# A seven-product MLP on one Trainium2 core: second products onto a seeded PSUM bank, inner products that end by themselves, sums of w1 loaded by GpSimd

## The chip, the cores and the metric

The kernel runs on one core of one Trainium2 chip. The metric is the time of one execution in microseconds (us) on the device, over several runs. PE is TensorE (the matrix engine, PEld its weight loads), DVE is VectorE, ACT is ScalarE, POOL is GpSimd, SP is SyncE.

## The reference

Two blocks in a row, all in fp32. The first is a routed attention (4 batches, 8 heads, 768 rows, 64 columns a head, 16 clusters). The change touches only the second, an MLP with a residual for each of the 3072 rows:

```python
# x: (4, 768, 512), the output of the attention block
mu = np.mean(x, axis=-1, keepdims=True)
var = np.mean((x - mu) ** 2, axis=-1, keepdims=True)
xn = (x - mu) / np.sqrt(var + 1e-06) * g_ln
ch = np.maximum(xn @ w_ch1, 0.0) @ w_ch2     # 512 -> 2048 -> 512
return (x + ch).astype(np.float32)
```

## The kernel before

**Products.** Each matrix product of the MLP is cut into 2 x 2 blocks and done with seven products of blocks in place of eight, on sums of blocks (the scheme of Strassen and Winograd). The code calls the products "ways" or "parts" 1 to 7. Their results are put together so: block (0,0) is 1 + 2; a chain 1, 6, 7, 4 is accumulated in the PSUM bank `x`, and copied out after each step (p1, u2, u3, and the end, which is block (1,0)); 5 is in the bank `z`; block (1,1) is z + u3; 3 is accumulated onto z, and block (0,1) is z + u2. Product 2 has a bank `y` of its own, and `add_relu` (L913) or `put_in` (L1227) adds the kept p1 to it on DVE.

**Stages.** By the times of the trace: attention to 317.4 us. Batch 0 goes through the first layer to 387.3 and through a plain second layer to 462.5. Batch 1 has its first layer to 531.1; its second is "deep" to 600.6: the seven products are themselves made of seven each, 49 products (`deep_product`, L1200) of four matmuls of 192 columns. Batches 2 and 3 have a "paired" first layer (`paired_layer`, L1473; to 666.6 and 799) and a deep second layer (to 733.5 and about 862.5). The first layer's products are `first_layer` (L926), four matmul records of 384 columns each. Some of them are done by pairs of blocks with seven inner products of one matmul of 192 columns (`inner_products`, L1334); in the paired layer there are three kinds, called A, B and C in the plan, for the first, fifth and third sum.

**Order.** All of it stands in an order written out by hand for each engine (`manual_schedule`). For the first layer the tuple `parts` (L1778) gives the order of the parts of a block with what is put between them; for the deep layer `STEPS` (L1056) walks `ORDER` (4, 7, 1, 6, 5, 2, 3), and for each m the ways 1, 2, then 4 and 3 of the m before, then 6, 5, 7. The jobs that a step carries (row norms of the next batch, transposes and stores of results, ring loads of weights on SP) are hung on pairs (way, slot) and (m, way).

**PSUM and buffers.** After the attention the banks are a pool of six for `x` and `z` and one of two for the rest. The copies p1, u2, u3 of the chain are in `hid`, tag "p", five buffers. ReLU is a separate ACT instruction on what DVE has added (`relu`, L921).

**w1.** `w1_sums` (L666) makes the four sums of blocks of w1 on DVE for batch 0 and for batch 1, four adds for each of eight blocks. Batch 0's are also written to DRAM (`outer_keep`, L1373, array `w1_all`), from where the later batches load them.

## Time and profile before

| | us |
|---|---|
| runs | 872.70, 870.51, 872.72 |
| median of the runs | 872.70 |
| the profiled execution's own time | 870.29 |
| its span, first to last instruction | 868.7 |
| granted clock of PE in it | 0.999 of full |

The span is what the rows below speak of; the 1.6 us between it and the execution's own time lie around it. Times in rows are counted from the start of the span.

### The profile page before, as it was taken

Reading aid. Unit: us, or ns where it says so; the run is one execution under the profiler, and the core shown is the slowest. Engines: PE = TensorE matmul, PEld = TensorE weight load, DVE = VectorE, ACT = ScalarE, POOL = GpSimd, SP = SyncE. Lnnn points to the kernel's source line nnn. Section 1 sums busy time; section 2 is a strip of 40 time slices with the busy share of each in tenths; the row PEclk is TensorE's granted clock in tenths of the full one; section 3 lists DMA queues with packets and bytes.
Section 4 is the critical chain, followed back from the end, with each engine's and each line's share of the span. In section 5 each row is a group of like instructions: output and inputs, shape, how many; then the busy total and the mean of one; then the engine's idle time right before and its main releaser. Section 6 shows DMA issues by size and latency. Waiting matters only on the chain.

```text
span 868.7 us, 13931 instructions
## 1 busy us (share of the span) xinstructions
PE 861.5 (99%) x4827; PEld 597.5 (69%) x4827; DVE 740.1 (85%) x1304; ACT 425.9 (49%) x808; POOL 142.5 (16%) x230
## 2 busy tenths in 40 slices
PE   8999999999999999999999999999999999999997
PEld 5444444444444446668887667998778999778997
DVE  6899999999999878888977898888888897767876
ACT  6877788888888845561003543112663111344110
POOL 2011221222222223220000210002430002250000
PEclk9999999999999999999999999999999999999999
DMA  8777889999976428978695788965556975464866
GB/s 169 137 128 130 143 177 191 201 207 202 196 168 188 126 100 262 277 189 312 204 272 153 227 272 240 293 199 172 160 151 212 343 202 166 129 169 145 275 202 124
DMA packets 229866, 169.63 MB, mean 195 GB/s; under 512 B 159440, under 2 KB 180448, under 8 KB 228768
## 3 DMA queue, kind: packets, MB, share of 16 engines
q1 hardware_dynamic: 193344, 140.30, 58.8%
q0 software_dynamic: 11632, 23.95, 12.7%
q10 hardware_dynamic: 24816, 4.45, 2.9%
q8 instruction: 39, 0.64, 0.3%
q14 instruction: 35, 0.29, 0.1%
HBM read 119.67 MB, written 40.59 MB: 184 GB/s over the span
## 4 chain that ended last, share of the span: by engine, by line
PE 97%; DVE 1%; DMA 1%; issue 0%; ACT 0%; SPq 0%; ACTq 0%; DVEq 0%
PE x_ps L881 19%; PE s_ps L420 18%; PE a_ps L432 15%; PE x_ps L1216 12%; PE z_ps L1216 6%; PE x_ps L998 5%; PE z_ps L881 5%; PE x_ps L1342 5%; PE y_ps L1216 3%; PE z_ps L998 2%; PE z_ps L1342 2%; PE sim_ps L331 2%; PE den_ps L488 1%; PE y_ps L998 1%; PE y_ps L1342 1%; PE y_ps L881 1%
## 5 line engine op out<-in xcount | busy, mean ns | idle before, releaser
L420 PE MATMUL s_ps<-t,t 64*128 64x384 f32 x768 | 155.0, 483 | 0.1
L420 PEld LDWEIGHTS s_ps<-t,t 64*128 64x128 f32 x768 | 67.9, 187 | 39.1 <-issue 38.3
L1291 POOL DMA_DIRECT2D out_dram<-y x64 | 49.6, 783 | 209.1 <-DVE y L1277 183.6
L1216 PE MATMUL x_ps<-lower,w 128*128 128x192 f32 x448 | 80.5, 326 | 0.0
L1216 PEld LDWEIGHTS x_ps<-lower,w 128*128 128x128 f32 x448 | 74.2, 190 | 0.8
L412 ACT ACTIVATE e<-s_ps 128x768 f32<-128x768 f32 x83 | 66.4, 812 | 7.2 <-PE s_ps L420 6.6
L412 ACT ACTIVATE w<-s_ps 128x768 f32<-128x768 f32 x80 | 64.4, 812 | 7.9 <-PE s_ps L420 7.0
L420 PE MATMUL s_ps<-mask,mask 64*128 64x384 bf16 x384 | 62.3, 323 | 0.4 <-ACT e L412 0.4
L923 ACT ACTIVATE lower<-lower 128x384 f32<-128x384 f32 x88 | 42.9, 520 | 35.5 <-DVE lower L915 30.5
L910 ACT COPY p<-x_ps 128x384 f32<-128x384 f32 x31 | 14.7, 475 | 92.5 <-PE x_ps L881 85.6
L432 PE MATMUL a_ps<-e,v_sb 128*64 128x384 f32 x336 | 57.6, 488 | 0.0
L432 PE MATMUL a_ps<-w,v_sb 128*64 128x384 f32 x320 | 55.2, 488 | 0.0
L881 PE MATMUL x_ps<-xn,w 128*128 128x384 f32 x128 | 46.6, 487 | 0.0
L881 PE MATMUL x_ps<-xn,ws 128*128 128x384 f32 x128 | 46.6, 487 | 0.0
L881 PE MATMUL x_ps<-xt,w 128*128 128x384 f32 x128 | 46.5, 486 | 0.0
L881 PE MATMUL x_ps<-xt,ws 128*128 128x384 f32 x128 | 46.4, 486 | 0.0
L432 PEld LDWEIGHTS a_ps<-e,v_sb 128*64 128x64 f32 x336 | 23.5, 137 | 31.8 <-issue 28.7
L432 PEld LDWEIGHTS a_ps<-w,v_sb 128*64 128x64 f32 x320 | 22.4, 137 | 30.4 <-issue 27.3
L300 POOL DMA_DIRECT2D w<-tb x32 | 29.1, 908 | 80.9 <-DVE tb L297 64.4
L420 PEld LDWEIGHTS <-mask 64*128 64x128 bf16 x384 | 18.9, 94 | 33.9 <-issue 10.9
L1229 ACT COPY u<-x_ps 128x192 f32<-128x192 f32 x30 | 9.6, 319 | 65.9 <-PE x_ps L1216 61.3
L377 ACT ACTIVATE mask<-oh,far 32x384 bf16<-32x384 bf16 x61 | 37.3, 612 | 3.3 <-DVE oh L360 1.9
(346 smaller groups left out, 1893.3 us busy)
## 6 DMA issues: line engine op xcount, KB each, us to landing
w<-w_d SPq DMA_DIRECT2D x84, 256.0 KB, 3.5
raw<-in_moe_w_ch_dram SPq DMA_DIRECT2D x32, 512.0 KB, 4.9
w<-w_t SPq DMA_DIRECT2D x36, 256.0 KB, 5.0
w<-tb POOLq DMA_DIRECT2D x32, 256.0 KB, 5.4
w<-w_all SPq DMA_DIRECT2D x27, 256.0 KB, 3.5
v_sb<-in_v_dram SPq DMA_DIRECT2D x32, 192.0 KB, 3.3
xr<-x_d SPq DMA_DIRECT2D x24, 256.0 KB, 3.6
q_sb<-in_q_dram SPq DMA_DIRECT2D x62, 96.0 KB, 4.1
```

The costliest lines, as they stand in the source:

```text
L300: nc.gpsimd.dma_start(out=w, in_=fb, accum_op=ALU.add)
L331: nc.tensor.matmul(sim[r : r + Q, :HC], cT[:, pr, :, :].rearrange("p j c -> p (j c)"), prepared[n][side][:, g * HC : (g + 1) * HC], start= ...
L377: nc.scalar.activation(out, oh[src, :], AF.Identity, bias=add, scale=factor)
L412: nc.scalar.activation(e, s[2][:, :, :HC], AF.Exp, scale=SCALE)
L420: nc.tensor.matmul(s[j][:, :HC], of_keys[:, keys], of_queries[:, o : o + HC], start=part == first, stop=part != first, skip_group_check=True,)
L432: nc.tensor.matmul(acc[j * D : (j + 1) * D, :HC], loaded[n]["v"][:, j, c, :], e[:, j, :], start=(c == 0), stop=(c == NT - 1),)
L881: nc.tensor.matmul(bank[:, :HC], lhs[:, c, :], rhs[:, c], start=first and c == 0, stop=c == NDH - 1, skip_group_check=True,)
L923: nc.scalar.activation(h, h, AF.Relu)
L998: nc.tensor.matmul(bank[:, :MH].rearrange("p (h f) -> p h f", h=2), hidden[lhs + (c,)][:, tt * P : (tt + 1) * P], rhs[:, :, c], start=firs ...
L1216: nc.tensor.matmul(bank, w[:, c, :], a[:, c], start=(way in (1, 2, 5) or alone) and c == 0, stop=c == NQH - 1, skip_group_check=True,)
L1291: queues[i % len(queues)].dma_start(out=to, in_=y)
L1342: nc.tensor.matmul(bank, p["w"][way], p["x"][way], start=way in (1, 2, 5), stop=True, skip_group_check=True)
```

## The change

- Product 2 no longer has a bank of its own. A bank `seed` (pool of one) is opened once, by two bf16 matmuls that write it. After that, product 1 is copied into it (ACT; DVE adds into it where a further term belongs to it), and product 2 is accumulated onto that without a start flag. The result leaves with a copy or a ReLU on ACT. The other banks are three for `x` and four for the rest.
- In the deep layer the order of the ways becomes 1, 4 of the m before, 2, 3 of the m before, 6, 5, 7; in the first layer 4 of the block before moves ahead of 2.
- Inner products get their own sum: the block's p1 is kept in one tile for the pair (`first_kept`), the seven inner products end in the hidden tiles with ACT copies and two DVE adds, and one DVE add of 768 columns (`add_kept`) puts p1 on afterwards. In batch 3 the first two groups of the kind C still add onto what is there (`onto`), by DVE into the seed.
- For batch 1 the sums of w1 are loaded from `w1_all` on GpSimd's queue (`w1_room`, `w1_back`) instead of being made on DVE.
- `hid` "p" has three buffers, not five; `between` moves from step (4, 2) to (4, 1).

```diff
@@ PSUM pools, opening of the seed
-    pools["long"], pools["t"] = pool("ps_m", 6, space=PSUM), pool("ps_n", 2, space=PSUM)
+    seeds = pool("ps_k", 1, space=PSUM)
+    pools["chain"], pools["t"] = pool("ps_m", 3, space=PSUM), pool("ps_n", 4, space=PSUM)
+    def seeded(n):
+        return seeds.tile([P, 512], F32, tag="seed", name="seed_ps")[:, :n]
+    def open_seeded():
+        bank, parts = seeded(4 * P), ident.bitcast(BF16)
+        for i in range(2):
+            nc.tensor.matmul(
+                bank[:, i * 2 * P : (i + 1) * 2 * P], parts[:, :P], parts,
+                start=i == 0, stop=True, skip_group_check=True,
+            )
@@ first_kept, add_kept
+    def first_kept(j):
+        if j % 2 == 0:
+            ones_of["t"] = hid.tile([P, 2, HC], F32, tag="pp", name="p1", bufs=1)
+        return ones_of["t"][:, j % 2]
+    def add_kept(r, l, j, t):
+        h = place((r, l))[:, j : j + 2].rearrange("p c t -> p (c t)")
+        nc.vector.tensor_tensor(h, h, t, ALU.add)
+        summed.extend(hidden_tile(r, l * NFH + j + i) for i in range(2))
@@ first_layer
-            st["p1"] = kept(st["x"], "p1", None if b or j else w2[:, NFC - 6, :HC])
+            if j < FROM.get(b, 0):
+                st["y"] = seeded(HC)
+                nc.scalar.copy(st["y"], st["x"][:, :HC])
+            else:
+                kept(st["x"], "p1", first_kept(j))
         elif part == 2:
-            y = ps("y_ps")
-            product(y, w1_block(0, 1, j), x_block(b, 1, 0), True)
-            add_relu(0, j, y, st["p1"])
+            product(st["y"], w1_block(0, 1, j), x_block(b, 1, 0), False)
+            nc.scalar.activation(hidden_tile(0, j), st["y"], AF.Relu)
@@ STEPS
-        for way in (1, 2, 4, 3, 6, 5, 7):
-            if way not in (3, 4):
-                STEPS.append((m, way))
-            elif before:
-                STEPS.append((before, way))
+        for way in (1, 4, 2, 3, 6, 5, 7) if before else (1, 5, 6, 2, 7):
+            STEPS.append((before if way in (3, 4) else m, way))
@@ deep_product
         if way == 1:
-            kept_sum("p1", 0, 0)
+            p["y"] = seeded(QC)
+            put_in(rows_of(p["y"]), part(p["add"], 0, 0))
         elif way == 2:
-            put_in(part(p["to"], 0, 0), p["p1"])
+            put_in(part(p["to"], 0, 0), None)
@@ inner_products
+            if way == 1:
+                p["in", "y"] = seeded(QC)
...
+            if way == 1:
+                put_in(p["in", "y"], 0, 0)
+            elif way == 2:
+                nc.scalar.copy(p["to"](*at[way]), bank)
+            elif way == 4:
+                put_in(p["to"](*at[way]), *at[way])
+            elif way in (6, 7):
+                p["kept", way] = p["keep"](way)
+                put_in(p["kept", way], *{6: (0, 1), 7: (1, 1)}[way])
+            if way in (7, 3):
+                onto = p["kept", {7: 7, 3: 6}[way]]
+                nc.vector.tensor_tensor(p["to"](*at[way]), p["in", "z"], onto, ALU.add)
+    INNER = {1: (1,), 2: (2, 6, 5), 3: (7,), 4: (4, 3)}
@@ sums of w1 of batch 1, and the order of the first layer
+    def w1_back(b, j, a=0, z=4):
+        if j < NFH:
+            n = NDH * P
+            t = sets[b, j]["all"].rearrange("p s k f -> p (s k f)")
+            nc.gpsimd.dma_start(out=t[:, a * n : z * n], in_=w1_all[j, :, a * n : z * n])
...
-        parts, sums_after, inner_at = ((1, 0), (2, 0), (4, 1), (6, 0), (3, 1), (5, 0), (7, 0)), 5, {}
+        parts, sums_after, inner_at = ((1, 0), (4, 1), (2, 0), (6, 0), (3, 1), (5, 0), (7, 0)), 5, {}
...
-            inner_at = {5: (7,), 6: (4, 3)} if j % 2 else {6: (1, 2), 7: (6, 5)}
+            inner_at = {5: INNER[3], 6: INNER[4]} if j % 2 else {6: INNER[1], 7: INNER[2]}
...
-                    summed.extend(hidden_tile(0, j - i) for i in (1, 0))
+                    add_kept(0, 0, j - 1, flat(ones_of["t"]))
...
+            if b and j and part in (1, 7):
+                w1_back(b, j + 1, *{1: (0, 3), 7: (3, 4)}[part])
-            if part == (sums_after if j or b == 0 else 6) and j + 1 < NFH:
+            if b == 0 and part == sums_after and j + 1 < NFH:
                 w1_sums(b, j + 1)
```

In the rows of orders below, the number behind a name tells buffers apart; `in_ps` is a bank of inner products, `p1` the pair's kept tile, `pi` and `kept` are copies of inner products.

DVE where batch 1 goes from its first into its deep second layer, before (`z_ps_4537` and `z_ps_4597` are the z banks of the last two blocks, `wt` are sums of w2, `qs` inner sums):

```order
L1351 TENSOR_TENSOR lower_3195<-x_ps_4548,p1_4595 128x192
L1357 TENSOR_TENSOR lower_3195<-z_ps_4570,pi_4174 128x192
L1106 TENSOR_TENSOR wt_4576<-w2_t_4461 128x512
L1106 TENSOR_TENSOR wt_4576<-w2_t_4461,wt_4576 128x512
L915 TENSOR_TENSOR lower_3195<-z_ps_4537,u2_4546 128x384
L1164 TENSOR_TENSOR fifth_3690<-lower_3195 128x384
L1166 TENSOR_TENSOR lower_3195<-lower_3195 128x384
L1168 TENSOR_TENSOR w2_158<-fifth_3690,lower_3195 128x384
L915 TENSOR_TENSOR lower_3195<-z_ps_4597,u3_4629 128x384
```

And after:

```order
L1403 TENSOR_TENSOR lower_3198<-in_ps_4548,pi_4176 128x192 x2
L949 TENSOR_TENSOR lower_3198<-lower_3198,p1_4513 128x768
L1145 TENSOR_TENSOR wt_4555<-w2_t_4446 128x512
L1145 TENSOR_TENSOR wt_4555<-w2_t_4446,wt_4555 128x512
L954 TENSOR_TENSOR lower_3198<-z_ps_4520,u2_4529 128x384
L1203 TENSOR_TENSOR fifth_3693<-lower_3198 128x384
L1205 TENSOR_TENSOR lower_3198<-lower_3198 128x384
L1207 TENSOR_TENSOR w2_158<-fifth_3693,lower_3198 128x384
L954 TENSOR_TENSOR lower_3198<-z_ps_4575,u3_4608 128x384
```

`add_kept` (L949) now stands ahead of a pair of sums `wt` and of the add onto z, and one small add (L1351) is gone.

DVE in the first group of batch 3's paired layer, before (`x_ps_6102` is the inner bank of C's products 1, 6, 7, 4, and `a3_6014` is the room in which its product 1 is kept):

```order
L1546 TENSOR_TENSOR lower_3195<-qs_6028,lower_3195 128x768
L1351 TENSOR_TENSOR lower_3195<-x_ps_6059,p1_6037 128x192
L1357 TENSOR_TENSOR lower_3195<-z_ps_6071,pi_6033 128x192
L1351 TENSOR_TENSOR a3_6014<-x_ps_6102,lower_3195 128x192
L1357 TENSOR_TENSOR lower_3195<-y_ps_6105,a3_6014 128x192
L1546 TENSOR_TENSOR lower_3195<-qs_6028,lower_3195 128x768
```

And after (`in_ps_6065` takes the place of `x_ps_6102`):

```order
L1602 TENSOR_TENSOR lower_3198<-qs_5992,lower_3198 128x768
L1403 TENSOR_TENSOR lower_3198<-in_ps_6033,pi_5997 128x192
L949 TENSOR_TENSOR lower_3198<-lower_3198,p1_5971 128x768
L1388 TENSOR_TENSOR seed_ps_6067<-in_ps_6065,lower_3198 128x192
L1602 TENSOR_TENSOR lower_3198<-qs_5992,lower_3198 128x768
L1388 TENSOR_TENSOR pi_5997<-in_ps_6065,lower_3198 128x192 x2
```

C's product 1 goes into the seed, by an add that stands behind the add of 768 columns.

PE at the last m of batch 3's deep layer, before (`x_ps_6816` is that m's chain, `x_ps_6750` the chain of the m before):

```order
L1216 MATMUL x_ps_6750<-lower_3195,w2_158 128x192 x4
L1216 MATMUL x_ps_6816<-lower_3195,w2_158 128x192 x4
L1216 MATMUL y_ps_6828<-lower_3195,w2_158 128x192 x4
L1216 MATMUL x_ps_6750<-lower_3195,w2_158 128x192 x4
L1216 MATMUL z_ps_6798<-lower_3195,w2_158 128x192 x4
```

And after (`x_ps_6773` and `x_ps_6708` are the same chains):

```order
L1253 MATMUL x_ps_6708<-lower_3198,w2_158 128x192 x4
L1253 MATMUL x_ps_6773<-lower_3198,w2_158 128x192 x4
L1253 MATMUL x_ps_6708<-lower_3198,w2_158 128x192 x4
L1253 MATMUL seed_ps_6778<-lower_3198,w2_158 128x192 x4
L1253 MATMUL z_ps_6755<-lower_3198,w2_158 128x192 x4
```

Way 4 of the m before has moved between ways 1 and 2, and way 2 is in the seed. DVE there, before:

```order
L1231 TENSOR_TENSOR u3_6810<-x_ps_6750,m1_6583 128x192
L1231 TENSOR_TENSOR m1_6583<-z_ps_6798,u3_6810 128x6x32
L1188 TENSOR_TENSOR lower_3195<-lower_3195 128x24x32
L1277 STREAM_TRANSPOSE y_6814<-m7_6526 128x768
L1231 TENSOR_TENSOR p1_6821<-x_ps_6816,m5_6694 128x192
L1193 TENSOR_TENSOR lower_3195<-qs_6028,lower_3195 128x24x32
L1231 TENSOR_TENSOR m5_6694<-y_ps_6828,p1_6821 128x6x32
```

And after:

```order
L1268 TENSOR_TENSOR u3_6767<-x_ps_6708,m1_6544 128x192
L1268 TENSOR_TENSOR m1_6544<-z_ps_6755,u3_6767 128x6x32
L1227 TENSOR_TENSOR lower_3198<-lower_3198 128x24x32
L1315 STREAM_TRANSPOSE y_6771<-m7_6488 128x768
L1268 TENSOR_TENSOR seed_ps_6778<-x_ps_6773,m5_6653 128x192
L1232 TENSOR_TENSOR lower_3198<-qs_5992,lower_3198 128x24x32
L1268 TENSOR_TENSOR m1_6544<-x_ps_6708,m1_6544 128x6x32
```

The add of way 1 keeps its place behind the transpose of 768 columns, and now writes the seed instead of `p1`.

## Rows read from the trace of the kernel before

**Rows 1.** The page: span, busy time by engine, last chain by engine.

```profile
span 868.7 us, 13931 instructions
...
PE 861.5 (99%) x4827; PEld 597.5 (69%) x4827; DVE 740.1 (85%) x1304; ACT 425.9 (49%) x808; POOL 142.5 (16%) x230
...
PE 97%; DVE 1%; DMA 1%; issue 0%; ACT 0%; SPq 0%; ACTq 0%; DVEq 0%
```

**Rows 2.** The waits of PE: line, what for, total us, times, longest.

```profile
PE idle_ps L717 <- DVE warm L176: 1.3, 1, 1.3
PE turned L1658 <- ACT y_end L1660: 0.5, 1, 0.5
```

**Rows 3.** Stages: length, busy PE, PEld, DVE, ACT, POOL, clock, DMA share, GB/s.

```profile
317.40:387.30 69.90, 69.90 (x243) 43.53 (x244) 57.86 (x133) 40.06 (x87) 17.19 (x24) 1.00 0.81 230
...
462.50:531.10 68.60, 68.60 (x243) 44.06 (x243) 55.86 (x137) 34.70 (x84) 8.63 (x12) 1.00 0.74 224
...
733.50:799.00 65.50, 65.50 (x287) 49.43 (x286) 46.49 (x101) 28.10 (x68) 18.61 (x24) 1.00 0.48 140
```

**Rows 4.** DVE groups from 317.4 us: count, busy us, mean ns, idle before.

```profile
L678 DVE TENSOR_TENSOR ws<-w 128x256 f32<-128x256 f32 x30 | 12.5, 417 | 0.0
...
L1357 DVE TENSOR_TENSOR lower<-z_ps,pi 128x192 f32<-128x192 f32 x34 | 12.1, 355 | 0.7
...
L1546 DVE TENSOR_TENSOR lower<-qs,lower 128x768 f32<-128x768 f32 x12 | 11.4, 947 | 0.0
```

**Rows 5.** ACT groups from 317.4 us, in the same columns.

```profile
L910 ACT COPY p<-x_ps 128x384 f32<-128x384 f32 x31 | 14.7, 475 | 92.5 <-PE x_ps L881 85.6 <-DVE qs L1309 6.8
...
L594 ACT ACTIVATE xr<-xr,mv 128x512 f32<-128x512 f32 x12 | 8.7, 722 | 0.4
...
L1353 ACT COPY kept<-x_ps 128x192 f32<-128x192 f32 x24 | 7.7, 320 | 6.1 <-PE x_ps L1342 5.5 <-DVE lower L1546 0.6
```

**Rows 6.** Timeline near 620: start, duration, engine, instruction.

```profile
619.84 0.32 ACT L1353 COPY kept<-x_ps 128x192 f32<-128x192 f32 x1
...
620.21 0.30 PEld L1342 LDWEIGHTS x_ps<-qs,ws 128*128 128x128 f32 x2 [0.44 <-ACT kept L1353]
```

**Rows 7.** Timeline where batch 1 goes into its second layer.

```profile
531.00 1.46 PE L1216 MATMUL x_ps<-lower,w 128*128 128x192 f32 x8
...
531.25 0.48 ACT L910 COPY u<-x_ps 128x384 f32<-128x384 f32 x1
...
532.30 1.13 PE L881 MATMUL x_ps<-xt,w 128*128 128x384 f32 x3
...
535.56 0.35 DVE L1186 TENSOR_TENSOR qs<-lower 128x192 f32<-128x192 f32 x1
```

**Rows 8.** Timeline of the first group of batch 3.

```profile
742.57 0.95 DVE L1546 TENSOR_TENSOR lower<-qs,lower 128x768 f32<-128x768 f32 x1
...
743.10 1.45 PE L881 MATMUL x_ps<-xt,w 128*128 128x384 f32 x4
...
743.71 0.35 DVE L1357 TENSOR_TENSOR lower<-z_ps,pi 128x192 f32<-128x192 f32 x1
...
744.39 0.58 PE L1342 MATMUL x_ps<-qs,w_in 128*128 128x192 f32 x2
```

**Rows 9.** Timeline of the last block, end of batch 3.

```profile
852.13 1.46 PE L1216 MATMUL y_ps<-lower,w 128*128 128x192 f32 x8
852.87 0.97 DVE L1277 STREAM_TRANSPOSE y<-m 128x768 f32<-128x768 f32 x1
...
853.43 1.14 PE L1216 MATMUL x_ps<-lower,w 128*128 128x192 f32 x6
853.76 0.32 DVE L1231 TENSOR_TENSOR p<-x_ps,m 128x192 f32<-128x192 f32 x1
```

**Rows 10.** DMA issues between 600 and 800: count, KB each, us to landing.

```profile
ws<-w_all SPq DMA_DIRECT2D x7, 512.0 KB, 4.0
```

More of the change, by code (lines that the diff above doesn't have):

```diff
@@ L74, in ps @@
     def ps(name, dt=F32, n=512):
-        p = pools["long" if "long" in pools and name in ("x_ps", "z_ps") else "t"]
+        p = pools["chain" if "chain" in pools and name == "x_ps" else "t"]
         return p.tile([P, n], dt, tag="t", name=name)
@@ L678, in w1_sums, with w1_room @@
                 nc.vector.tensor_tensor(t[:, i], x, y, op)
+    def w1_room(b):
+        rooms = [xpool.tile([P, 4, NDH, P], F32, tag="ws", name="ws", bufs=2) for _ in range(2)]
+        for j in range(NFH):
+            t = rooms[j % 2]
+            sets[b, j] = {"s": [t[:, i] for i in range(4)], "all": t}
+    def w1_back(b, j, a=0, z=4):
[3 more added lines that the diff above has]
+            nc.gpsimd.dma_start(out=t[:, a * n : z * n], in_=w1_all[j, :, a * n : z * n])
     extra = {}
@@ L1217, in deep_product @@
                 bank, w[:, c, :], a[:, c],
-                start=(way in (1, 2, 5) or alone) and c == 0, stop=c == NQH - 1, skip_group_check=True,
+                start=(way in (1, 5) or alone) and c == 0, stop=c == NQH - 1, skip_group_check=True,
             )
@@ L1368, in second_pair @@
             "w": w, "x": x, "keep": keep_in(parts),
-            "onto": lambda r, h: sets[b, j + r]["p1"][:, half[h]],
             "to": lambda r, h: hidden_tile(0, j + r)[:, half[h]],
@@ L1380, in pair_begin @@
             pool = splits if b else pools["conv"]
-            t = pool.tile([P, 3 * QC], F32, name="pi")
-            pairs_of["parts"] = [t[:, i * QC : (i + 1) * QC] for i in range(3)]
+            t = pool.tile([P, 2 * QC], F32, name="pi")
+            pairs_of["parts"] = [t[:, i * QC : (i + 1) * QC] for i in range(2)]
             x = x_block(b, 1, 0)
@@ L1480, in paired_layer @@
         t = flat(unit("pi"))
-        second = [t[:, i * QC : (i + 1) * QC] for i in range(3)]
+        second, third = [[t[:, i * QC : (i + 1) * QC] for i in range(m, m + 2)] for m in (0, 2)]
+        third_sum = []
         if last:
-            third = [w_in["a3"][:, 2 * QC + i * QC : 3 * QC + i * QC] for i in range(2)] + [t[:, 3 * QC :]]
             sums_of = {2: w_in[2], 5: w_in[5][:, 4 * P :], 3: w_in[3]}
@@ L1512, in first_of @@
             return {
-                "w": w_operands(a11, a12, a22, parts_of(sums_of[5], 4)), "x": x_of[5], "onto": None,
-                "keep": lambda way: hid.tile([P, HC], F32, tag="p", name="kept", bufs=5)[:, :QC],
+                "w": w_operands(a11, a12, a22, parts_of(sums_of[5], 4)), "x": x_of[5],
+                "keep": lambda way: hid.tile([P, HC], F32, tag="p", name="kept", bufs=3)[:, :QC],
                 "to": lambda r, h: fifth_sum[:, r * HC + h * QC : r * HC + (h + 1) * QC],
@@ L1518, in third_of @@
         def third_of(g):
+            alone = g >= (2 if last else THIRD)
+            if alone and not third_sum:
+                third_sum.append(flat(unit("third")))
             def to(r, h):
-                return hidden_tile(1, 2 * g + r)[:, half[h]]
+                if not alone:
+                    return hidden_tile(1, 2 * g + r)[:, half[h]]
+                return third_sum[0][:, r * HC + h * QC : r * HC + (h + 1) * QC]
             if last:
@@ L1526, in third_of @@
                 w = w_operands(a11, a12, a22, [p for t in ends for p in parts_of(t, 2)])
-            return {"w": w, "x": x_of[3], "onto": to, "to": to, "keep": keep_in(third)}
+            return {"w": w, "x": x_of[3], "to": to, "onto": None if alone else to, "keep": keep_in(third)}
         def second_of(g):
@@ L1539, in steps @@
                 state[what, g] = makers[what](g)
-            inner_products(state[what, g], {1: (1, 2), 2: (6, 5), 3: (7,), 4: (4, 3)}[i])
-            if i == 4 and what != "B":
-                summed.extend(hidden_tile(int(what == "C"), 2 * g + r) for r in range(2))
+            inner_products(state[what, g], INNER[i])
+            if i == 4 and what == "A":
+                add_kept(0, 0, 2 * g, flat(ones_of["t"]))
+            elif i == 4 and what == "C" and state[what, g]["onto"]:
+                summed.extend(hidden_tile(1, 2 * g + r) for r in range(2))
+            elif i == 4 and what == "C":
+                add_kept(1, 0, 2 * g, third_sum[0])
         def onto_first(j, l):
@@ L1596, in paired_layer @@
                     if g == THIRD and slot == 2:
-                        t = flat(unit("third"))
-                        third.extend(t[:, i * QC : (i + 1) * QC] for i in range(3))
                         x_of[3] = inner_x(x_block(b, 1, 1), flat(unit("x3")))
```

52 lines of the change are left out of this document (22 added, 30 removed).

## The prediction

> **What bounds the kernel now.** I read the head of the page and the chain of waits first [rows 1]: TensorE (PE) is busy 861.5 of 868.7 us, and the chain that ends last is 97% PE work. VectorE (DVE) has 85%, ScalarE (ACT) 49%. Next the list of what PE waited for [rows 2]. It has six entries, 3.1 us together, and every one lies in the first 16 us or after the last product; the two rows shown are the longest and one at the end. Then the table by stage [rows 3]: in every stage from 16 to 847 us PE's busy time equals the length of the stage. So in the stages that the change edits, PE is never late. The four batches' products simply follow each other, and the time is their sum. A change of DVE's or ACT's load is worth nothing there unless it removes PE work (this one doesn't) or makes PE wait (which it can). A gain could come only from the 7.2 us in which PE is idle, at both ends.
>
> **PE's work.** The number and the shapes of the products are the same before and after; product 2 gets no start flag and lands in another bank, that is all. The only new PE work is two bf16 matmuls of 256 columns before the first product. Their price is not in the trace. From below it is 0; from above it is two fp32 matmuls of 256 columns, which by the deep product of four 192-column matmuls in 1.30 us (852.13 to 853.43, [rows 9]) cost 1.30/4 x 256/192 = 0.43 each, 0.9 together. I take 0.2, as fp32 is the dearer type. The same place gets a new order (product 5 before 2, the attention's last relu ahead of the seed copy on ACT); I add 0.2 there, between 0 and one copy of 0.475. **Start: 0.4.**
>
> **What is taken from DVE.** Per pair of inner products five DVE adds of 192 columns (0.355 each, [rows 4]) go, 1.8 us, and one add of 768 (0.95, L1546's size) comes. In batch 1, DVE loses the 32 sums of w1 (0.417 each, 13.3 us, half of the 60 in that stretch with its two other forms, [rows 4]) and GpSimd loads them instead. By rows 2 and 3 PE did not wait for any of these, so their removal is priced at nothing, unless it repairs a wait made by the rest of the change.
>
> **What is added as a wait.** Product 2 can't start before product 1 has been copied into the seed bank, and between them now lies one product (1.29 us in the first layer: 743.10 to 744.39, [rows 8]; 1.30 in the second). The order of the ways is 1, 4 of the block before, 2, and product 7's copy before product 4 has one product of cover too, where two stood. What a cover must hold: an evacuation starts about 0.25 us after the product's end (531.00 to 531.25, [rows 7]), takes 0.475 (384 columns) or 0.32 (192, [rows 5]), and PE goes on 0.05 after it (kept ends at 620.16, the weight load starts at 620.21, [rows 6]). That is 0.78 of 1.29 and 0.62 of 1.30. So 0.5 to 0.7 us are spare: one instruction ahead on ACT (0.5) is hidden, a DVE add of 768 (0.95) or a row norm on ACT (L594, 0.72) with a copy behind it is not. By the order of the changed kernel about 100 of PE's waits have no more cover than that, against some 47 before. I went through those behind which a long instruction stands. ACT's bursts in batch 0 (it is busy 40 of 70 us there, [rows 3]) fall between copies, so no term comes from there.
>
> No row of before shows ACT writing to PSUM. I price the seed copy like the copy to SBUF, 0.475 and 0.32; the bounds are 0.25 less and 0.25 more, which moves only the terms on ACT. The Trainium skill ("ScalarE: Activation LUTs", section "Step-by-step: what each stage is for") says that ScalarE reaches PSUM faster than SBUF. No run here shows it yet; by it the batch 2 term below would be smaller, and the sum nearer to 3.8.
>
> The places, in the trace's own times:
> - **Batch 1, into its second layer.** The 0.95 add stands ahead of two weight sums and of an add onto z that the relu waits for, while one 0.35 add is gone: DVE is 0.6 late, the relu behind it too, and the u copy (531.25 before) ends near 532.4, with PE due at 532.30 [rows 7]: 0.1 to 0.3, take 0.2. Product 5 of the block is moved up to directly after the old product 3 and needs the last quarter of its sum. That ended at 535.91 (535.56 + 0.35, [rows 7]) and now ends 0.6 later, at 536.5; PE's fourth matmul of that product is due after two first-layer products and three matmuls, 532.30 + 2 x 1.29 + 0.98 + 0.2 (the wait before) = 536.06: 0.45. Together **0.65**.
> - **Batches 2 and 3, into the second layer.** The same add ahead of the inner sums, and products 5 and 6 due earlier: 0.3 and 0.25, **0.55**.
> - **Batch 2, first layer.** ACT gets five copies more per group, behind row norms. At 620 the copy before the release had 0.06 to spare (it ends at 620.16, the weight load follows at 620.21, [rows 6]); one copy of 0.32 more makes it 0.25 to 0.3 late. Two such places, and 0.1 for smaller ones: **0.7**.
> - **Batch 3, first layer.** The third's product 2 waits for an add that DVE makes into the seed. DVE: L1546 ends 743.52, L1357 to 743.8, the new 768 add to 744.75, the seed add to 745.05, PE 745.1. PE comes 0.33 earlier than before, since one 192 product less stands ahead: 744.39 - 0.33 = 744.06 [rows 8]. So 1.0; the next group, where DVE has less in front, 0.3. **1.3**.
> - **The end.** In the last block DVE transposes (852.87, 0.97) before it adds p (853.76 to 854.08). PE needed that result only two products later; now the seed add must be done at 853.43: **0.7** [rows 9].
>
> Waits on PE add up: everything behind shifts. 0.4 + 0.65 + 0.55 + 0.7 + 1.3 + 0.7 = 4.3 us. Against the profiled execution's own 870.29 that is 874.6. That execution is near the lowest of the runs shown (870.51); two of three stand at 872.7, which makes 877.0. I take the middle, **876**. If every ACT and DVE price were right and PE's waits overlapped with slack won elsewhere, 2 to 3 of the 4.3 would remain; if the bounds all go the bad way, about 9, twice the sum.
>
> **GpSimd's loads.** Fourteen transfers, 4 MB in 70 us, 60 GB/s on top of 224 at a DMA share of 0.74 [rows 3]: the share goes to about 0.94. Such a load takes 4.0 us for 512 KB on another queue [rows 10]; each is issued at least 6 us ahead, so I price it at 0. Behind GpSimd's wait for the room stand only the turned columns, with long lead.
>
> **The rivals.**
> 1. *The covers hold.* DVE has lost more than it got, ACT is idle half the time, and a wait of 0.3 vanishes if a copy starts 0.3 earlier. For it: before, no wait of 47 with short cover cost anything [rows 2]. Against: the batch 3 and the end term rest on 0.95 instructions that nothing moves. Then only the start is left, +0.4: 870.7 on the lower level, 873.1 on the upper, about 872. Chance 0.27.
> 2. *Lag everywhere.* If ACT's copy into PSUM takes 0.25 longer than to SBUF, or the release is slower than 0.05, spare falls to about 0.3 and half of the 100 waits lose some 0.2: +10, 884. It decides from a seed copy of about 0.7 on. No row speaks for it. Chance 0.07.
> 3. *Loads of w1 late.* At a share of 0.94 the 4.0 us could double and pass the 6 us of lead; eight blocks late by 1 us each give 882. Against: earlier stages ran at 0.81 without a wait [rows 3]. Chance 0.04.
> 4. *Faster.* PE's busy time could hide room: the weight loads (PEld) fill only 69% of the span [rows 1], and if the products had gaps between them that DVE's adds cause, taking 13 us and more off DVE would close some, a few us: 868 and lower. It decides if the pitch of the products falls below 1.29. Against: that pitch is the same at every place that I looked at, and the idle time is 7.2 us, none of it in the edited stages. The Trainium skill ("Perfetto Trace Analysis", section "Identifying the Most-Contended Engine") judges PE's headroom by the share of its weight loads, not by its busy time. By that rule there would be room here; the constant pitch speaks against reading it so. Chance 0.04.
>
> **How the numbers follow.** The forecast has 0.58. About 0.3%, 2.6 us, is what a measurement of this kernel can tell from no change. Of the forecast's case some 0.05 fall inside that. Faster 0.04 (rival 4); within 0.27 + 0.05 = 0.32, rounded with rival 1's tail to 0.33; slower 0.53 + 0.07 + 0.04 = 0.64, rounded to 0.63. The range goes from rival 1's lower level, 871, to the forecast with doubled waits on the upper level, 872.7 + 9 = 882; it leaves out rival 4 and most of 2.
>
> **What the profile of the changed kernel will show.** Right: PE waits in the list that weren't there, "seed <- DVE" near 744 and 853 and "<- ACT" near 620, 0.3 to 1.0 us each, some ten of them, 4 to 5 us together, and stages of batches 2 and 3 longer than PE's busy time in them. Rival 1: the list has the old six entries and no stage is longer than before by more than 0.3. Rival 2: dozens of entries below 0.3. Rival 3: "ws <- DMA" between 462 and 531. The forecast is wrong if the batch 3 first layer (65.5 us) is not longer by about 1.3, or if a stage gets shorter.

## The result, and the profile after

| us | before | after |
|---|---|---|
| median of the runs | 871.61 (870.47 to 872.72, 4 runs) | 880.99 (880.46 to 883.23, 4 runs) |
| the profiled execution's own time | 870.29 | 881.35 |
| first to last product of the MLP | 545.07 | 555.25 |
| last product to the end of the span | 6.37 | 6.81 |

The ratio is 1.0113 (95% interval 1.0087 to 1.0138): slower, by 9.4 us in the medians and 11.1 in the two profiled executions. The time ahead of the MLP differs by up to 1.8 us between the traces of this case (the MLP's first product starts between 317.29 and 319.07), and most of that difference stands already at the attention's first scores product (8.94 to 10.51). So below, runs are compared by the MLP part, and places by the start of the same product in two traces: how much later it starts than in the kernel before is called its lag.

The head of the page, after:

```profile
span 879.8 us, 13958 instructions
...
PE 867.6 (99%) x4829; PEld 597.3 (68%) x4829; DVE 709.5 (81%) x1159; ACT 457.8 (52%) x939; POOL 150.3 (17%) x244
```

Against [rows 1], DVE is relieved of 31 us, ACT has 32 more, and PE has the same 2588 matmuls in the MLP. But its busy time has grown by 6 us, although only two small matmuls came in. The list of PE's waits, after (line, what for, total us, times, longest us):

```profile
PE seed_ps L1380 <- DVE seed_ps L1388: 1.1, 2, 0.9
PE x_ps L907 <- ACT seed_ps L975: 0.8, 1, 0.8
PE x_ps L907 <- ACT p L936: 0.8, 1, 0.8
PE z_ps L907 <- DVE ws L678: 0.7, 1, 0.7
PE seed_ps L1253 <- DVE seed_ps L1268: 0.6, 1, 0.6
...
PE x_ps L1253 <- issue: 0.4, 2, 0.2
...
PE in_ps L1380 <- DVE qs L1403: 0.3, 1, 0.3
PE x_ps L907 <- ACT u L936: 0.2, 1, 0.2
PE z_ps L907 <- DVE lower L954: 0.2, 1, 0.2
```

None of these nine was in the list before, whose six entries lie at the two ends [rows 2]. The table by stage, after, with the columns of [rows 3] (the eight stages of the MLP, cut at the shifted times):

```profile
317.74:388.70 70.96, 69.52 (x242) 42.84 (x241) 54.60 (x119) 42.30 (x100) 16.91 (x24) 1.00 0.79 226
...
465.20:536.30 71.10, 70.20 (x248) 44.38 (x247) 44.45 (x92) 38.80 (x104) 15.26 (x24) 1.00 0.81 258
...
742.00:809.00 67.00, 65.87 (x289) 49.66 (x288) 39.47 (x68) 36.73 (x103) 18.62 (x24) 1.00 0.45 137
...
sum 554.96, PE 549.67 PEld 446.30 DVE 416.36 ACT 200.44 POOL 82.96; mean PE 68.71 PEld 55.79 DVE 52.04 ACT 25.06 POOL 10.37
```

Before, busy PE equalled the length in every stage [rows 3]. Now 554.96 - 549.67 = 5.3 us are idle. That is only half of the loss of 10.2; the other half stands as busy time. A wait costs more than the list shows, by two amounts that rows give:

- A record is longer than the pitch: product 471.10 (below) has a record of 1.45 and the next starts 1.29 later. So the first 0.16 us of any wait lie under the old record.
- The four matmuls of a product that PE waited for take longer: 1.56 in place of 1.45, about 0.10 more.

After, timeline at the start of batch 1 (start, duration, engine, instruction, idle time before with its releaser):

```profile
455.54 11.98 ACTq L540 DMA_DIRECT2D x_d<-turned  x8
467.56 0.48 ACT L936 COPY p<-x_ps 128x384 f32<-128x384 f32 x1 [40.50 <-DMA out_dram<-o_sb]
...
468.09 1.56 PE L907 MATMUL x_ps<-xt,ws 128*128 128x384 f32 x4 [0.75 <-ACT p L936]
...
471.10 1.45 PE L907 MATMUL x_ps<-xn,ws 128*128 128x384 f32 x4
```

The idle 0.75 plus 0.16 plus 0.10 is 1.0 us of lag. The trace has 17 waits with idle time in the MLP, and 17 x 0.26 is 4.4 us; some eight shorter waits that lie wholly under an old record add a little. That is about the half that the list does not show (an estimate from these rows). Lag arises at these 25 or so places only; at the other 2560 matmuls PE keeps its pitch. Where the lag arose:

| up to the product that starts, in the kernel before, at | lag there | new | forecast |
|---|---|---|---|
| 317.7, start | 0.34 | 0.34 | 0.4 |
| 326.8, batch 0, second block | 1.36 | 1.02 | 0 |
| 387.3, end of batch 0's first layer | 2.26 | 0.90 | 0 |
| 475.3, start of batch 1 | 3.91 | 1.65 | 0 |
| 531.2, end of its first layer | 4.28 | 0.37 | 0 |
| 545.1, into its deep layer | 5.57 | 1.29 | 0.65 |
| 660.2, batch 2, first layer | 6.66 | 1.09 | 0.7 |
| 676.0 and 808.1, into the deep layers of batches 2 and 3 | 7.39 and 9.80 | 0.73 + 0.72 | 0.55 |
| 799.2, batch 3, first layer | 9.08 | 1.69 | 1.3 |
| 858.1, the last block | 10.63 | 0.83 | 0.7 |

### The profile page after: what moved, and what is told of

Its sections match the earlier page's. It is cut to its first block, busy times and chain, and to the rows that moved or that the text cites. A ratio compares the mean times of both kernels' runs of the same rounds, so it can differ in the third digit from the quotient of the medians.

```text
span 879.8 us, 13958 instructions
## 1 busy us (share of the span) xinstructions
PE 867.6 (99%) x4829; PEld 597.3 (68%) x4829; DVE 709.5 (81%) x1159; ACT 457.8 (52%) x939; POOL 150.3 (17%) x244
## 4 chain that ended last, share of the span: by engine, by line
PE 86%; DVE 7%; DMA 3%; POOL 1%; issue 1%; ACT 0%; SPq 0%; DVEq 0%; ACTq 0%
PE s_ps L420 18%; PE x_ps L907 16%; PE a_ps L432 14%; PE x_ps L1253 12%; PE z_ps L1253 6%; PE in_ps L1380 6%; PE z_ps L907 4%; PE seed_ps L1253 3%; PE sim_ps L331 2%; PE den_ps L488 1%; POOL out_dram L1329 1%; PE y_ps L1040 1%; PE x_ps L1040 1%; DMA xb<-x_d 1%; PE seed_ps L1380 1%; DMA xr<-x_d 1%
```

## The experiments

The theory: each lag has one releaser that stands too late in its engine's order, as in the forecast's sum, but at more places than the forecast looked at. The rivals: lag everywhere from covers that are too short or from ACT's writes to PSUM; and DVE's relief as a hidden gain that the rest eats up. All edits are to the changed kernel. Most were run once, and single runs of one kernel differ by 2 to 3 us (the table above), so what an edit does is read from the lag at its place and from the length of the MLP (first to last product, 555.25 in the changed kernel). The labels e1 to e12 name the runs.

**The second block of batch 0 (e4).** The list names ACT's seed copy for the wait of 0.8. The timeline there, after, says something else:

```profile
325.88 0.56 DVE L954 TENSOR_TENSOR lower<-z_ps,u 128x384 f32<-128x384 f32 x1 [3.64 <-ACT u L936]
326.36 0.95 DVE L662 TENSOR_TENSOR xt<-xn,xt 128x768 f32<-128x768 f32 x1
326.72 0.46 ACT L975 COPY seed_ps<-x_ps 128x384 f32<-128x384 f32 x1 [0.87 <-PE x_ps L907]
...
327.40 0.56 PE L907 MATMUL x_ps<-xt,w 128*128 128x384 f32 x1 [0.78 <-ACT seed_ps L975]
```

Product 4 reads `xt`, the fourth sum of x, and starts 0.09 after that add ends at 327.31; the seed copy, which it doesn't need, ended at 327.18. In the first layer 4 was moved ahead of 2, so it needs the sum one product earlier than before.

```diff
         first_layer(0, 0, 6)
+        x_sum(0, 4)
         finish(len(pairs) - 1, 0)
         first_layer(0, 0, 7)
-        x_sum(0, 4)
```

> The changed kernel, but the fourth sum of x of batch 0 (one 768-column subtraction, 0.95 us) stands on DVE ahead of the add onto z that waits for ScalarE, not behind it. Theory (operands, not evacuations): the wait of product 4 at 327.4 (0.94 and 0.07) is for that sum, since product 4 moved ahead of product 2; it vanishes, span 0.9 to 1.0 shorter. Rival (it waits for the copy into the seed, as the list of waits names it): nothing changes.

Measured: 881.48, and the lag of 1.02 is gone there. In this run product 4 starts ahead of the seed copy:

```profile
326.41 1.13 PE L907 MATMUL x_ps<-xt,w 128*128 128x384 f32 x3
326.66 0.46 ACT L975 COPY seed_ps<-x_ps 128x384 f32<-128x384 f32 x1 [0.86 <-PE x_ps L907]
```

The cause is the operand, not the seed. But the MLP did not get shorter (555.43): at the start of batch 1 PE waits 1.04 longer, for the reason given there.

**The sums of w1 in batch 0 (e6).** At 372.85 product 5 waits for `ws`, a sum of w1 that DVE makes behind add_kept (0.96) and the steps of a chunk of weights that is split in this batch. The edit puts the sums ahead of the chunk's steps.

```diff
+            if b == 0 and part == sums_after and j + 1 < NFH:
+                w1_sums(b, j + 1)
+                outer_keep(b, j + 1)
             if chunks and part in (5 if j >= FROM[b] else 2, 3):
...
                 join_weight(m)
...
-            if b == 0 and part == sums_after and j + 1 < NFH:
-                w1_sums(b, j + 1)
-                outer_keep(b, j + 1)
```

> The changed kernel, but in batch 0 DVE makes the next block's w1 sums ahead of the split weight chunk's last steps (0.42 + 0.69 us) and not behind them. Theory (DVE got one 768-column add more ahead of these sums): the wait of product 5 at 372.9 for them (0.82 and 0.07) vanishes, span 0.8 to 0.9 shorter. Rival (PE waits there for ScalarE): it stays.

Measured: 882.5; the wait for `ws` is gone, and the lag of 0.90 has become 0.49. In its place PE waits for the copy u, as the list of that run shows:

```profile
PE x_ps L907 <- ACT u L936: 0.4, 2, 0.2
```

So here the next thing in line takes half of what the edit frees. That the new add is what made `ws` late is read from the trace; the edit moved the chunk's steps, not the add.

**The start of batch 1, by elimination (e1, e5, e10).** Product 6 waits for the copy p. ACT is idle for 40 us before that copy, but its queue isn't: it issues eight transfers `x_d<-turned` until 467.52, each waiting for columns turned from a load. The same in the kernel before:

```profile
450.77 12.17 ACTq L540 DMA_DIRECT2D x_d<-turned  x8
463.82 0.48 ACT L910 COPY p<-x_ps 128x384 f32<-128x384 f32 x1 [39.02 <-PE x_ps L881]
```

There the last issue ended at 462.94, 0.9 before PE let the copy go. After, it ends 4.6 later, where PE has a lag of 2.3. The transfers issued between 434 and 452, before and then after (count, KB each, us to landing):

```profile
x_d<-turned ACTq DMA_DIRECT2D x10, 96.0 KB, 4.1
...
xb<-x_d SPq DMA_DIRECT2D x4, 128.0 KB, 3.1
```

```profile
ws<-w_all POOLq DMA_DIRECT2D x2, 512.0 KB, 7.9
x_d<-turned ACTq DMA_DIRECT2D x6, 96.0 KB, 7.8
...
xb<-x_d SPq DMA_DIRECT2D x4, 128.0 KB, 6.8
```

GpSimd's first two loads fall where the DMA engines were full already. Before and then after, the same window of 5 us (the last two columns are DMA share and GB/s):

```profile
445.00:450.00 5.00, 5.00 (x25) 4.41 (x24) 1.61 (x3) 0.00 (x0) 0.00 (x0) 1.00 1.00 191
```

```profile
445.00:450.00 5.00, 5.00 (x25) 4.41 (x24) 1.77 (x4) 0.00 (x0) 0.00 (x0) 1.00 1.00 308
```

From 455 to 460 the share had fallen to 0.72 before, and is still 0.96 after. That reads as a collision. The Trainium skill ("DMA: Bandwidth & Descriptors", section "Issuing engines are not separate DMA queues") says that transfers of all issuing engines end up on the same 16 DMA engines and interleave there; the landings on ACT's and SP's queues agree with it.

A first edit (e1) issues the two loads later and on SP's queue:

```diff
-    def w1_back(b, j, a=0, z=4):
+    def w1_back(b, j, a=0, z=4, queue=nc.gpsimd):
...
-                do(w1_room, 1), do(w1_back, 1, 0), do(w1_back, 1, 1),
+                do(w1_room, 1),
...
-            (3, 0): [do(x_sum, 1, 3)],
-            (3, 1): [do(x_sum, 1, 4)],
+            (3, 0): [do(x_sum, 1, 3), do(w1_back, 1, 0, 0, 4, nc.sync)],
+            (3, 1): [do(x_sum, 1, 4), do(w1_back, 1, 1, 0, 4, nc.sync)],
```

> The changed kernel, but GpSimd's first two loads of w1 sums (512 KB each, issued at 440.8 and 442.4 us in it) are issued by SyncE about 12 to 15 us later, where the DMA share is lower. Theory (single places): those two loads collide with the transposed columns of batch 1 (landing 7.8 us in place of 3), so ScalarE's queue is still issuing their stores when batch 1's product 1 ends, and PE waits 0.92 us at 468.1. Expected: that wait falls to 0.3 or less, the rest of the list unchanged, the span 0.7 to 1.2 us shorter. Rival (the chain to batch 1 is late because of DVE's new order in the second layer, not because of the loads): the wait stays at 0.7 to 0.9.

Measured: 884.08, and PE still waits 1.1 there. The expectation was missed, but the run settles nothing: the loads were now issued at 447.5, 5 to 7 us later and not 12 to 15, still in the full stretch (a share of 1.06 to 1.07 from 445 to 455), and the `x_d` transfers of that stretch landed in 9.1 us.

A second edit (e5) makes the sums of the first two blocks on DVE, as before the change, and drops only these two loads:

```diff
-        if 0 in which:
+        if 0 in which and (b, j) not in sets:
...
+            if b and j == 0 and part == 6:
+                w1_sums(b, 1)
...
-                do(w1_room, 1), do(w1_back, 1, 0), do(w1_back, 1, 1),
+                do(w1_room, 1),
...
-            (3, 1): [do(x_sum, 1, 4)],
+            (3, 1): [do(x_sum, 1, 4), do(w1_sums, 1, 0)],
```

> The changed kernel, but the w1 sums of batch 1's first two blocks are made by DVE (as in the kernel before), and GpSimd loads only those of the blocks from the third on, so 1 MB of loads leaves the stretch around 441 us. Theory (the loads take DMA time from the transposed columns, whose stores then hold ScalarE's queue): the wait of product 6 at the start of batch 1, 0.9 to 2.2 us in the runs so far, falls to 0.3 or less, since the stores end about 2.5 us earlier. Rival (the stores are late because all of batch 0 is, by its two waits of 1.0 and 0.9 us): it stays at 0.9 or more.

Measured: 880.5; the wait is gone and with it a shorter one for DVE at 473 (0.38), -1.40 of the 1.65 together, with 0.28 back a little later; the MLP takes 554.10. The timeline at the start of batch 1 in this run, and the transfers issued between 434 and 452:

```profile
466.51 0.48 ACT L936 COPY p<-x_ps 128x384 f32<-128x384 f32 x1 [39.02 <-PE x_ps L907]
...
467.60 1.45 PE L907 MATMUL x_ps<-xt,ws 128*128 128x384 f32 x4
```

```profile
x_d<-turned ACTq DMA_DIRECT2D x7, 96.0 KB, 4.3
```

The copy waits for PE again, and the landings are back near 4.1. So the two loads were the cause. PE's own lag in batch 0 is not: in e4 PE reached this place 1.07 earlier, and ACT's last transfer was issued at 467.49 all the same (467.52 in the changed kernel). The size of the wait in the changed kernel is not settled: over the runs that keep the loads its lag went from 0.9 to 2.5. Since ACT's transfers, not PE, set the time here, this wait hides what e2, e3, e4 and e6 won at their own places: their MLPs take 555.45, 557.27, 555.43 and 555.68, none less than 555.25. A placement of the loads outside the full stretch was not tried.

The third edit (e10) gives all of batch 1's sums back to DVE:

```diff
-            if b and j and part in (1, 7):
-                w1_back(b, j + 1, *{1: (0, 3), 7: (3, 4)}[part])
-            if b == 0 and part == sums_after and j + 1 < NFH:
+            if part == (sums_after if j or b == 0 else 6) and j + 1 < NFH:
                 w1_sums(b, j + 1)
-                outer_keep(b, j + 1)
+                if b == 0:
+                    outer_keep(b, j + 1)
...
-                do(w1_room, 1), do(w1_back, 1, 0), do(w1_back, 1, 1),
...
-            (3, 1): [do(x_sum, 1, 4)],
+            (3, 1): [do(x_sum, 1, 4), do(w1_sums, 1, 0)],
```

> The changed kernel with all w1 sums of batch 1 on DVE again, as in the kernel before: that part of the change undone, 4 MB of GpSimd loads out and 12 us of DVE adds back. Theory (DVE's relief there buys nothing, the loads cost): the waits at batch 1's start (1.4 us in the run shown, up to 2.8 in others) vanish, and no wait over 0.3 comes up between 475 and 535: 1.4 to 2.8 shorter. Rival (the relief pays, since DVE has the 768-column adds to make now): 0.5 to 2 us of new waits for DVE in batch 1, and the gain is at most half.

Measured: 880.85. The start is 1.40 better, but then 0.29, 0.89 and 0.24 are lost, the largest to a sum of w1 again:

```profile
PE z_ps L907 <- DVE ws L678: 1.3, 2, 0.7
```

(In the changed kernel that line has one wait, of 0.7.) The MLP takes 555.25, the same as with the loads; so the rival was right. The relief of DVE from the third block on is worth about 1.1 in the changed kernel (555.25 against 554.10 in e5), and the first two loads cost as much; the net is nothing. In the kernel before no wait for DVE stood there to be relieved.

**The first groups of batch 3 (e2).** C's seed add stands behind add_kept, as the forecast had it. After:

```profile
751.25 0.96 DVE L949 TENSOR_TENSOR lower<-lower,p 128x768 f32<-128x768 f32 x1
...
752.12 0.36 DVE L1388 TENSOR_TENSOR seed_ps<-in_ps,lower 128x192 f32<-128x192 f32 x1
...
752.54 0.59 PE L1380 MATMUL seed_ps<-xn,a 128*128 128x192 f32 x2 [0.92 <-DVE seed_ps L1388]
```

The edit puts add_kept behind the seed add:

```diff
-                add_kept(0, 0, 2 * g, flat(ones_of["t"]))
+                put_off.append((0, 0, 2 * g, flat(ones_of["t"])))
...
+                while put_off:
+                    add_kept(*put_off.pop(0))
```

> The changed kernel, but in batch 3's paired layer the DVE add into C's seed stands ahead of the 768-column add that puts p1 on. Theory (single places): the two waits of PE for the seed (1.08 and 0.38 us with their restart) vanish and the span is 1.4 to 1.6 us shorter. Rival (the seed itself is slow, by the write into PSUM and the release): 0.5 or more of them stays.

Measured: 881.75; the first group's 1.07 is gone, the second's 0.38 is not. In the second group add_kept belongs to a slot further ahead, which the edit doesn't reach. In this run the add comes first:

```profile
752.51 0.36 DVE L1388 TENSOR_TENSOR seed_ps<-in_ps,lower 128x192 f32<-128x192 f32 x1
752.77 0.95 DVE L949 TENSOR_TENSOR lower<-lower,p 128x768 f32<-128x768 f32 x1
```

**The last block (e3).** After, the place of [rows 9]:

```profile
862.67 0.97 DVE L1315 STREAM_TRANSPOSE y<-m 128x768 f32<-128x768 f32 x1
863.56 0.33 DVE L1268 TENSOR_TENSOR seed_ps<-x_ps,m 128x192 f32<-128x192 f32 x1
...
863.95 1.24 PE L1253 MATMUL seed_ps<-lower,w 128*128 128x192 f32 x6 [0.55 <-DVE seed_ps L1268]
```

The edit puts the transpose behind the seed add:

```diff
-            jobs[2, 7].append(out_of(1, 1, 7))
+            jobs[3, 1] = [out_of(1, 1, 7)]
```

> The changed kernel, but in the last block the 768-column transpose of the result stands behind the add into the seed instead of ahead of it. Theory (single places): the wait at 863.9 (0.72 and 0.10 for the restart) vanishes; the span is 0.6 to 0.8 shorter, unless the transposed rows, stored up to 1 us later, become the end. Rival (the seed itself is slow): 0.3 or more of the wait stays.

Measured: -0.82 at that place, the transpose off the path. The time was 883.53 all the same, since this run's wait at the start of batch 1 was 2.2, and a slower clock followed it (last section).

**The covers (e7, e8).** Is one product of cover short, so that every place loses a little? Two edits measure the price of none and the spare of one. First (e7), way 2 directly behind way 1:

```diff
-        for way in (1, 4, 2, 3, 6, 5, 7) if before else (1, 5, 6, 2, 7):
+        for way in (1, 2, 4, 3, 6, 5, 7) if before else (1, 5, 6, 2, 7):
```

> The changed kernel with the deep layer's order of before (1, 2, 4, 3, 6, 5, 7): product 2 stands directly behind product 1, so each seed copy is uncovered. It measures the handshake itself, at 18 places (six of the seven m of three deep layers). By the prediction's price (0.25 + 0.32 + 0.05 = 0.62) and the 0.17 by which PE restarts late: 0.7 to 0.8 each, 13 to 14 us in all. By the rival that a copy into PSUM or its release is slow (0.9 and more): over 18 us. If the copy into PSUM is quicker than to SBUF by 0.1: 11 to 12.

Measured: 898.63. One of the places, in the timeline of this run:

```profile
559.76 0.30 ACT L1266 COPY seed_ps<-x_ps 128x192 f32<-128x192 f32 x1 [1.04 <-PE x_ps L1253]
...
560.12 1.57 PE L1253 MATMUL seed_ps<-lower,w 128*128 128x192 f32 x8 [0.45 <-ACT seed_ps L1266]
```

The idle 0.45 with the two hidden parts of 0.16 and 0.10 is 0.71 a place, at the 12 places where ACT copies; the forecast's arithmetic for such a cover, 0.62, is right but for the 0.10. Where DVE adds into the seed (the other six) a place loses 0.9 or more. The deep layers lose 4.7 to 5.1 each. A copy by ACT into PSUM takes 0.30 here, against 0.32 into SBUF [rows 5]: the dearer write that "lag everywhere" needed does not exist. (The sentence of the Trainium skill that the prediction cites from "ScalarE: Activation LUTs", section "Step-by-step: what each stage is for", says that ScalarE reaches PSUM faster; it holds by 0.02 us.)

Second (e8), the covers kept, but three more copies of 192 ahead of each of ACT's seed copies in the deep layers:

```diff
+            if p["add"] is None:
+                for i in range(3):
+                    nc.scalar.copy(hid.tile([P, HC], F32, tag="p", name="more", bufs=3)[:, :QC], bank)
```

> The changed kernel with three idle ScalarE copies of 192 columns (0.32 each) ahead of each ScalarE seed copy of the deep layers, 15 places, three of them with more cover. It measures the spare part of the cover: by the prediction 1.30 - 0.62 = 0.68, so 0.96 more makes product 2 wait 0.28, with the restart 0.45, at 12 places: +5 to 6 us. If the 100 short covers are already used up (rival: lag everywhere): +0.96 at each, 11 us and more.

Measured: 882.92; 0.14 lost in each deep layer and 0.33 at two of their starts, not the 5 to 6 expected. The timeline shows why:

```profile
556.76 0.76 ACT L1278 COPY more<-x_ps 128x192 f32<-128x192 f32 x3 [0.98 <-PE x_ps L1253]
...
557.39 0.35 ACT L1266 COPY seed_ps<-x_ps 128x192 f32<-128x192 f32 x1
```

Three copies push the seed copy back by 0.63, not 3 x 0.32: copies in a row overlap. (The Trainium skill, "ScalarE: Activation LUTs", section "What ACT_TABLE_LOAD costs", says that back-to-back ACTIVATEs overlap by about 93 ns; for these copies 3 x 0.32 - 0.76 is 0.20 for two overlaps, so the trace agrees.) So the spare of a cover in the deep layers is about 0.6, as the forecast had it (0.68). The first layers' covers were not edited, but the trace of the changed kernel itself shows lag at some 25 places and none at the rest. So "lag everywhere" is out: the covers hold, and the waits are single places.

**The starts of the deep layers (e9).** Where there is no m before, the order is 1, 5, 6, 2, 7. At the starts of batches 2 and 3 product 6 waits for an inner sum that DVE makes (L1232). The list names no releaser ("issue"), but the first of the two adds in the line below ends at 676.27, and the seed copy had ended at 675.93:

```profile
675.72 1.02 DVE L1232 TENSOR_TENSOR fifth<-qs,fifth 128x384 f32<-128x384 f32 x2
...
676.38 0.89 PE L1253 MATMUL x_ps<-fifth,w 128*128 128x192 f32 x4 [0.19 <-issue]
```

The edit puts 2 ahead of 6:

```diff
-        for way in (1, 4, 2, 3, 6, 5, 7) if before else (1, 5, 6, 2, 7):
+        for way in (1, 4, 2, 3, 6, 5, 7) if before else (1, 5, 2, 6, 7):
```

> The changed kernel, but the first m of each deep layer takes its ways as 1, 5, 2, 6, 7, so product 6 comes one product later. Theory (the deep layers start late because products 5 and 6 need their inner sums earlier): the waits before product 6 in batches 2 and 3 (0.35 and 0.07 each, at 676.4 and 811.2) vanish, those in product 5 (0.2 and 0.1 each) stay; 0.8 shorter in all, batch 1 unchanged. Rival (PE waits there for the copy of product 1): nothing changes, or product 2 waits in its place.

Measured: 882.75. The wait ahead of 6 is gone, and 2 doesn't wait for the seed copy in its place; but 7 now follows 6 directly and waits for the copy u of 6 at each of the three starts. In the list of this run:

```profile
PE x_ps L1253 <- ACT u L1266: 1.2, 3, 0.4
```

The net is a loss of 0.67, 0.31 and 0.31. The order of the changed kernel is the better one here.

**The edits together.** First all six (e11: e2, e3, e4, e5, e6 and e9 at once), then the five without e9 (e12):

> The changed kernel with six mends together: w1 sums of batch 1's first two blocks on DVE, the fourth sum of x and the next w1 sums of batch 0 earlier on DVE, C's seed ahead of the 768-column add, the last block's seed ahead of the transpose, product 2 ahead of 6 at the start of a deep layer. Theory (each wait is of its own place, and they add): 1.4 + 1.0 + 0.4 + 1.1 + 0.8 + 0.8 = 5.5 us less than the changed kernel, 874.5 to 876, still slower than before by 3 to 5, since PE's work is the same and about four waits remain (into batch 1's deep layer 1.3, batch 2's first layer 1.1, batch 3's second group 0.5, product 5 twice 0.3). Rival (a mend only moves the wait to the next instruction): 878 or more. If the seed scheme were a gain by itself: below 871.

> The changed kernel with five of the six mends: without the one that puts product 2 ahead of 6 (which left product 7 directly behind 6, 0.41 us of new wait at three places). Theory (each wait is of its own place): 0.9 to 1.2 us less than the version with six, 877.4 to 878; against the changed kernel 1.4 + 1.0 + 0.4 + 1.1 + 0.8 - 0.3 = 4.4 less in its profile from the start of the MLP on; still slower than before by 5 to 6 (0.6 to 0.7%), since before has none of the waits that remain. Rival (the seed scheme pays once its waits are gone): within 0.3% of before.

Measured: six, 878.78 (5 runs), ratio to the kernel before 1.0083 (1.0069 to 1.0097); five, 878.49 (6 runs), 1.0079 (1.0065 to 1.0093). With six, the expected 874.5 to 876 was missed: the MLP takes 552.09, 3.2 less than in the changed kernel and not 5.5, since e9's edit costs 1.3 where 0.8 of gain was expected, and half of e6's gain is lost again. With five, the MLP takes 550.79, 4.46 less than in the changed kernel (4.4 expected), though the time lies 0.5 above the expected 877.4 to 878. With the loads out of the way, the single gains add up. From the list of PE's waits of that run:

```profile
PE x_ps L907 <- ACT u L936: 0.5, 2, 0.2
```

The five large waits are gone; no single wait of the MLP in that list is over 0.2. What stays, 5.7 us in the MLP, is the way into the deep layers (1.29, 0.73 and 0.73), batch 2's first layer (1.07), some 0.9 in batch 1's, 0.6 in batch 3's and 0.49 in batch 0's; these were read from the trace and not tested by edits. The tail behind the last product is also longer in this run, 7.84 against 6.37; why stays open. So no version here beats the kernel before: with the large waits mended, the scheme still gives PE nothing to gain.

## Why the prediction came out as it did

The time lies in the range and on the side that had the largest chance, but the forecast had less than half of the loss: 4.3 us against 10.2 in the MLP. That the range held is in part luck: its upper end allowed for all foreseen waits doubling, and 3.6 of the missing 5.9 came from places that the sum held at 0.

- **What bounds the kernel: right.** PE was never late in the kernel before, so relief of DVE brought nothing and every new wait counted in full. DVE fell from 740 to 710 us, and no stage got shorter.
- **The places of the sum: right, most sizes low.** Lag arises at all of them. Batch 3's first layer (1.69 for 1.3) and the end (0.83 for 0.7) are near; e2 and e3 confirm the instruction that was named for each, e2 for the first group only. The start (0.34 for 0.4) is near by luck: 0.21 of it stands already at the attention's first scores product (9.18 for 8.97). The opening matmuls take 0.23 (317.51 to 317.74; 0.2 forecast), the new order costs nothing (0.2 forecast), and the first product no longer loses 0.10 to a restart. The way into the deep layers is two to three times the size (1.29 for 0.65, and 1.45 for 0.55): there each late step is followed by another, at 536.97, 538.73 and 541.32 in batch 1, and the forecast took 0.55 for both later batches together, where each of them pays about 0.73.
- **Batch 2's first layer: 1.09 for 0.7, half of it by another engine.** The copy that the forecast named, an ACT copy behind a row norm, makes PE late at 626.05 (0.09 idle, 0.4 of lag). The larger wait (0.5 of lag) is for DVE: the new add of 768 columns stands ahead of the add that makes an operand. Both are read from the trace; no edit tested them.

```profile
641.53 0.96 DVE L949 TENSOR_TENSOR lower<-lower,third 128x768 f32<-128x768 f32 x1
...
642.82 0.59 PE L1380 MATMUL in_ps<-xt,qs 128*128 128x192 f32 x2 [0.25 <-DVE qs L1403]
```

- **The mis-sized term: the wait itself.** The sum counted the time from when PE was due to when it was released. PE then loses about 0.10 more on the four matmuls behind the wait. With twelve waits with idle time at the foreseen places that is about 1.2 of the 2.4 us by which they came out dearer (6.7 in place of 4.3).
- **The failed step: "I went through those behind which a long instruction stands."** It went through evacuations alone, the covers. The three places priced at 0 in batches 0 and 1 (1.02, 0.90 and 1.65) are of another kind: an operand that DVE makes (the sum of x in e4, the sum of w1 in e6) is needed one product earlier or made one long add later, and a copy stands in ACT's order behind transfers that it issues (e5). "ACT's bursts in batch 0 fall between copies, so no term comes from there" was true of ACT and missed DVE.
- **GpSimd's loads at 0: wrong.** The argument took the mean DMA share of batch 1's first layer (0.74, and 0.94 forecast with the loads; it became 0.81) and the loads' own lead. But the first two loads are issued earlier, in a stretch with a share of 1.0, and what they made late was not themselves but other queues' transfers, on which ACT's order hangs (e5). Rival 3 had the collision, with the wrong victim.
- **Rival 1, the covers hold:** true of the covers (e8), yet not enough, since the losses are elsewhere. **Rival 2, lag everywhere:** refuted by e7 and e8 for the deep layers, and by the few places of lag in the trace for the others. **Rival 4, faster:** refuted; PE's pitch stayed 1.29. The Trainium skill ("Perfetto Trace Analysis", section "Identifying the Most-Contended Engine"), which the prediction weighed, judges PE's headroom by the share of its weight loads (beside the FLOPs used, which no row here gives). By that share, 68%, there would be room; here neither 31 us less on DVE nor the mending of the five largest waits brought PE below the time before.

## What to carry to other kernels

Where one engine is busy throughout and each product just follows the last, price an edit by the waits it makes on that engine alone, and price each wait at its gap plus a restart. When a product is moved ahead, look at all that it needs, not only the bank: the operands that another engine makes, and for each the instructions and the transfer issues that stand ahead in that engine's order. A load added where the DMA share is 1.0 is not free however long its own lead is; look for who else is landing there.

## What was not expected of the hardware

- A wait of PE costs 0.26 us beyond the idle time that the profile lists: 0.16 under the end of the record before it, 0.10 on the matmuls after it (1.56 for 1.45; at some places 0.07).
- The list of waits can name the wrong releaser: at 327.40 it names ACT's seed copy, which had been done for 0.2 us; the add of DVE that ended 0.09 before was the cause.
- In a stretch at a DMA share of 1.0, another 1 MB raised the median landing time of 96 KB transfers from 4.1 to 7.8 us (4.3 without it in e5).
- ACT's copies of 192 columns have a pitch of 0.21 us in a row, not their 0.32 (e8).
- After the longer wait of e3 at the start of batch 1 the granted clock fell for about 3 us to the lower of its two levels (0.51, 1.2 in place of 2.4 GHz). That run's windows:

```profile
467.00:470.00 3.00, 0.98 (x2) 0.38 (x2) 0.67 (x2) 0.48 (x1) 0.00 (x0) 0.92 0.63 151
470.00:473.00 3.00, 3.00 (x7) 1.99 (x6) 0.36 (x1) 0.66 (x2) 0.00 (x0) 0.51 0.73 196
```

The PE had been idle 2.0 us before, and so it had in e2 (0.99 busy of the same 3 us), where the clock stayed at 1.00, as it did after 2.3 us of idle time in e7. The fall cost 1.6 us of lag in e3; what decides it stays open.
